# Rounding 64-bit weights in the first block: the sum of the fraction's two parts, by GpSimd instead of VectorE

## The chip, the core and the metric

The kernel runs on one core of a Trainium2 chip. The metric is the device time of one execution in microseconds (us). The kernel before takes 1938.52 us, the median of six runs between 1937.91 and 1939.37 us.

The engines have short names in the profile. PE is TensorE (matrix products), DVE is VectorE, ACT is ScalarE, POOL is GpSimd. SP only issues DMAs here. Each engine works through its own instructions strictly in the order in which the program lists them. An instruction that has to wait for another engine therefore holds up everything behind it on its own engine.

## What is computed

```python
def _attn_ref(x):                      # x: 8 x 3008 x 256, float32
    X = np.fft.fft(x, axis=1)
    X = np.fft.fft(X, axis=2)
    return X.real.astype(np.float32)

def _moe_ref(x, w_in, w_out):          # x: 24064 x 256, w_in: 256 x 2048, w_out: 2048 x 256
    h = x @ w_in
    r = np.maximum(h, 0.0)
    g = r * r
    return (g @ w_out).astype(np.float32)
```

The second function is applied to the first one's output. The two weight matrices are multiplied by a numpy scalar when they are made and so arrive as 64-bit floats. The kernel rounds them to 32-bit floats itself, on the chip.

## The kernel before

The Fourier transform along the 256 columns is folded into `w_in`: the kernel multiplies `w_in` by a cosine and a sine table once and keeps the products in `G1` and `G2`. The transform along the 3008 rows is made per batch (8 batches) with matrix products and folds; its results are `Pt`, `Qt` and `Et`.

The main loop has 384 steps: 8 batches, 6 blocks of 251 (the last 250) columns, and 8 steps j in each block, for 8 pairs of 128 rows of the hidden layer. A step `i` does this:

- `front` (L664 to L670): for each half h, PE makes two products `ph` (L664, L665); DVE adds a term `he` (L667, with `gE`, a factor for each hidden row) and forms the sum and the difference in `g` (L669, L670).
- `combine`: ACT squares the positive part of `g` (L679, L680). From the second block on, POOL also forms four sums `s` (L687 to L690).
- `back`, for step `i-2`: PE multiplies by `wout` (L704 in the first block, L717 later). It needs `wout` of that step in its rounded form.

The first block (steps 0 to 7) also prepares the weights, one slice of `w_in` and one of `w_out` (each 128 x 512 values) per step, because all later blocks reuse them. This is `weights()`, which with `begin_win`, `load_wout` and `leftover` writes the order out by hand. In step `i` the engines get, after the `front` of that step:

1. PE: the products `pg` of `w_in` slice `i+1` with the two tables (L290); ACT copies them to `G1` and `G2` (L291).
2. The first half of rounding (`convert`) for `w_out` slice `i-1`.
3. The second half (`finish`) for `w_in` slice `i+2`, called by `rounded`.
4. The first half for `w_in` slice `i+3`, by `begin_win`.
5. The second half for `w_out` slice `i-1`, by `leftover`, and then `gE` for step `i+1` (L301), which DVE needs for the next step's `he`.

There are exceptions at the ends. Slices 0 and 1 of `w_in` are rounded before the loop. The first half of `w_in` slice 2 also starts there. In step 5 no more `w_in` begins. Step 6 rounds two `w_out` slices (5 and 6), and step 7 begins the last one, which step 8 finishes.

`convert` takes 64-bit floats as pairs of 32-bit words, `high` and `low`, which lie alternately in the tile `raw`. The first half cuts the exponent out of `high` (L262, DVE) and turns it into a 32-bit float's exponent (L264, L265, ACT), cuts the fraction's upper 20 bits out of `high` and sets the leading one (L267, DVE, to the tile `m`), and scales `low` to the fraction's lower part in place (L269, ACT). The second half puts the sign to the exponent (L272), adds the two parts of the fraction (L274) and multiplies fraction and exponent into the destination (L275), all on DVE. Tiles come from pools: three for `m`, two for the exponent, and six in three pools for `raw`. The load of a later slice into a `raw` tile waits until its last reader is done.

POOL's own queue holds, before the loop of the second block, only two DMA issues (L647, L648). They send a part of `Qt` round through DRAM into `Et`, which steps from the second block on use. `awake` is a row of idle matrix products that keeps PE busy during the start.

Of the kernel before, what the change touches and what calls it, by code (L numbers as in the profile page):

```python
# [11 lines left out]
ALU = mybir.AluOpType  # L12
# [70 lines left out]
def kernel(  # L83
# [12 lines left out]
    nc = tc.nc  # L96
# [27 lines left out]
    op = ctx.enter_context(tc.tile_pool(name="op", bufs=2))  # L124
# [5 lines left out]
    tt = nc.vector.tensor_tensor  # L130
# [70 lines left out]
    for i in range(2):  # L201
        nc.vector.tensor_scalar(out=signs[:, i:i + 1], in0=last, scalar1=(-2.0, 2.0)[i], scalar2=(1.0, -1.0)[i],
                                op0=ALU.mult, op1=ALU.add)
# [15 lines left out]
    def pair_in(j):  # L219

        return moe_w_in.rearrange("(c p) (h j f) -> j c p h f", p=P, j=NJ, h=2)[j]
# [5 lines left out]
    def parts(w, k):  # L227
        return w.rearrange("p c (e h) -> p h (c e)", h=k)
# [6 lines left out]
    def scratch():  # L235

        return sp.tile([P, 4 * CK], F32, name="m", tag="s")[:, 0:2 * CH].rearrange("p (c e) -> p c e", c=2)

    def load(src):

        nonlocal raws
        pool, tag = (gp, "g") if raws in (1, 2) else (xp, "x") if raws % (NX + 1) else (ep, "c")
        raws += 1
        single = src.dtype == F32
        raw = pool.tile([P, 2, CH, 1 if single else 2], src.dtype if single else U32, name="raw", tag=tag)
        for c in range(2):
            nc.sync.dma_start(out=raw[:, c].rearrange("p (o e) w -> p o (e w)", o=src.shape[2]),
                              in_=src[c] if single else src[c].bitcast(U32))
        return raw

    def convert(dst, raw):


        k = dst.shape[1]
        if raw.dtype == F32:
            return lambda: nc.vector.tensor_copy(dst, parts(raw[:, :, :, 0], k))
        low, high = raw[:, :, :, 0], raw[:, :, :, 1]
        m = scratch()
        e = fp.tile([P, 2, CH], F32, name="fd", tag="fd")
        mb, eb, rest = m.bitcast(U32), e.bitcast(U32), low.bitcast(F32)  # L260

        nc.vector.tensor_scalar(out=eb, in0=high, scalar1=20, scalar2=0x7FF,  # L262
                                op0=ALU.logical_shift_right, op1=ALU.bitwise_and)
        act(e, eb, AF.Relu, bias=ramp[:, 0:1], scale=-1.0)  # L264
        act(eb, e, AF.Relu, bias=ramp[:, 1:2], scale=-2.0 ** 23)  # L265

        nc.vector.tensor_scalar(out=mb, in0=high, scalar1=0xFFFFF, scalar2=0x100000,  # L267
                                op0=ALU.bitwise_and, op1=ALU.bitwise_or)
        act(rest, low, AF.Copy, scale=2.0 ** -32)  # L269

        def finish():
            nc.vector.scalar_tensor_tensor(out=eb, in0=high, scalar=0x80000000, in1=eb,  # L272
                                           op0=ALU.bitwise_and, op1=ALU.bitwise_or)
            tt(out=m, in0=mb, in1=rest, op=ALU.add)  # L274
            nc.vector.scalar_tensor_tensor(out=dst, in0=parts(m, k), scalar=2.0 ** -20, in1=parts(e, k),  # L275
                                           op0=ALU.mult, op1=ALU.mult)

        return finish


    def begin_win(j):

        w = ep.tile([P, 2, CH], F32, name="win", tag="sB" if j % 2 else "sA")
        finish = convert(parts(w, 1), win.pop(j, None) or load(pair_in(j)))

        def products():
            for tab, G, nm in ((cosd, G1, "mC"), (sind, G2, "mD")):
                pg = psm.tile([P, CH], F32, name="pg", tag=nm)
                for i in range(2):
                    nc.tensor.matmul(pg, tab[:, i], w[:, i], start=i == 0, stop=i == 1)  # L290
                nc.scalar.copy(G.rearrange("p (h j f) -> j p h f", h=2, j=NJ)[j],  # L291
                               pg.rearrange("p (h f) -> p h f", h=2))

        def for_e():

            ps = psd.tile([P, CH], F32, name="pe", tag="d")
            for h in range(2):
                fc = j + NJ * h
                nc.tensor.matmul(ps[:, h:h + 1], G2[:, fc * P:(fc + 1) * P], last, start=True, stop=True)

            return lambda: nc.vector.tensor_scalar_mul(gE[:, j::NJ], ps[:, 0:2], 0.5)  # L301

        win[j] = finish, products, for_e

    win = {}

    def load_wout(j):

        return convert(wout[:, j].rearrange("p h c e -> p h (c e)"), load(pair_out(j)))
# [533 lines left out]
    for_q(0)  # L843
    for_p(1)
    begin_win(0)
    load_x(0, 2)
    load_x(0, 3)
# [37 lines left out]
    q_part("odd0", "odd1", "odd2")  # L885
    copy_e = win[0][2]()
    begin_win(1)
    for_q(3)
    q_part("even0", "even1", "even2")
    awake(12)  # L890
    rounded(1)
    for kp in range(2):
        for nm in ("join_4", "join_2", "lo"):
            groups[1, kp, nm]()
        if kp == 0:
            begin_win(2)
# [44 lines left out]
    for i in range(len(steps) + LAG + 4):  # L941
        if i < len(steps):
            b, k0, n, j = steps[i]
# [96 lines left out]
```

## Time and profile before

| what | value |
|---|---|
| median of 6 runs | 1938.52 us |
| the profiled execution's own time | 1941.41 us |
| its span, first to last instruction | 1939.6 us |
| busy share of the span: PE, DVE, ACT, POOL | 99%, 73%, 48%, 61% |
| busy POOL instructions between 3.2 and 109.5 us | two DMA issues, 1.25 us |
| PE busy from 113.6 to 151.0 us (37.4 us long) | 37.40 us |
| mean granted TensorE clock | 0.997 of full speed |

The span is the distance from the first to the last instruction in one profiled execution; 1.8 us of that execution's own time lie outside it. A row of the timeline gives the start in us, the duration in us, the engine, the line of the code, the operation, the tiles and shapes (partitions x elements) and, in square brackets, how long the engine had stood idle before and what ended that. Durations of neighbours on one engine overlap a little: an instruction starts before the one ahead of it has drained. What an instruction takes away from its engine is therefore the distance from its start to the next start.

### The profile page before, as it was taken

How to read it: one execution, taken by the hardware profiler on the slowest of the kernel's cores; microseconds unless marked ns; L12 is line 12 of the kernel's file. 1: busy time of each engine (PE TensorE's matmuls, PEld its weight loads, DVE VectorE, ACT ScalarE, POOL GpSimd, SP SyncE). 2: the span in 40 equal slices, each digit the busy share in tenths (PEclk: the TensorE clock that was granted, in tenths of full speed). 3: DMA queues.
4: the chain of work that ended last, by engine and by line, in shares of the span. 5: the costliest groups of instructions: out<-in, count | busy, mean ns of one | idle time of the engine just before them, and what ended most of it. 6: DMA issues, size and time to landing. Idle time of an engine off the chain costs nothing.

```text
span 1939.6 us, 27913 instructions
## 1 busy us (share of the span) xinstructions
PE 1925.6 (99%) x9266; PEld 1711.9 (88%) x9266; DVE 1424.0 (73%) x3502; ACT 939.5 (48%) x1134; POOL 1184.1 (61%) x1708
## 2 busy tenths in 40 slices
PE   8999999999999999999999999999999999999999
PEld 7788888888988899888998889888898888988887
DVE  7998867777677876787667876777767787655554
ACT  2755544454445544544444454445544554444444
POOL 0047746776567665766566765666756676566655
PEclk9999999999999999999999999999999999999999
DMA  7332101111011100111011100111001100000000
GB/s 211 112 45 52 37 9 52 33 28 31 28 40 31 38 12 27 41 40 29 11 36 40 42 20 11 40 49 28 20 16 53 33 11 22 28 12 11 22 11 22
DMA packets 145783, 69.56 MB, mean 36 GB/s; under 512 B 129309, under 2 KB 136423, under 8 KB 145638
## 3 DMA queue, kind: packets, MB, share of 16 engines
q1 hardware_dynamic: 145186, 66.87, 13.3%
q8 instruction: 73, 1.20, 0.3%
q14 instruction: 72, 0.59, 0.1%
q0 software_dynamic: 176, 0.65, 0.1%
q10 hardware_dynamic: 276, 0.26, 0.0%
HBM read 43.03 MB, written 24.69 MB: 35 GB/s over the span
## 4 chain that ended last, share of the span: by engine, by line
PE 95%; DVE 3%; DMA 1%; issue 0%; SPq 0%; ACT 0%; DVEq 0%
PE ph L664 16%; PE ph L665 16%; PE mC L717 16%; PE mA L717 16%; PE mB L717 16%; PE mD L717 8%; PE pd L578 2%; PE pd L501 2%; DVE m L274 0%; DMA cosT<-in_cos_s_dram 0%; DMA sind<-in_sin_d_dram 0%; DVE he L667 0%; DVE fd L272 0%; DVE g L670 0%; PE mA L704 0%
## 5 line engine op out<-in xcount | busy, mean ns | idle before, releaser
L679 ACT ACTIVATE g<-g 128x1004 f32<-128x1004 f32 (+1 forms) x384 | 399.4, 1040 | 783.5 <-DVE g L670 424.4
L667 DVE SCALAR_TENSOR_TENSOR he<-Et,gE,ph 128x251 f32<-128x251 f32 (+1 forms) x768 | 361.6, 471 | 385.8 <-PE ph L665 382.7
L687 POOL TENSOR_TENSOR s<-g 128x251 f32<-128x251 f32 (+1 forms) x376 | 248.6, 661 | 641.9 <-ACT g L680 506.0
L664 PE MATMUL ph<-Pt,G 128*128 128x251 f32 (+1 forms) x1536 | 451.9, 375 | 0.2 <-DVE g L670 0.2
L665 PE MATMUL ph<-Qt,G 127*128 127x251 f32 (+1 forms) x1536 | 451.3, 374 | 0.0
L680 ACT ACTIVATE g<-g 128x1004 f32<-128x1004 f32 (+1 forms) x384 | 399.3, 1040 | 12.2
L717 PE MATMUL mC<-s,wsum 128*128 128x251 f32 (+1 forms) x1504 | 381.4, 374 | 0.0
L717 PE MATMUL mA<-g,wout 128*128 128x251 f32 (+1 forms) x1504 | 379.9, 374 | 0.0
L669 DVE TENSOR_TENSOR g<-he,ph 128x251 f32<-128x251 f32 (+1 forms) x768 | 320.6, 417 | 54.5 <-DVE he L667 0.9
L665 PEld LDWEIGHTS ph<-Qt,G 127*128 127x128 f32 x1536 | 291.3, 190 | 35.8
L664 PEld LDWEIGHTS ph<-Pt,G 128*128 128x128 f32 x1536 | 286.7, 189 | 36.2 <-DVE dc L547 1.3
L717 PEld LDWEIGHTS mC<-s,wsum 128*128 128x128 f32 x1504 | 285.5, 190 | 34.5
L670 DVE TENSOR_TENSOR g<-he,ph 128x251 f32<-128x251 f32 (+1 forms) x768 | 314.2, 409 | 0.0
L717 PEld LDWEIGHTS mA<-g,wout 128*128 128x128 f32 x1504 | 282.6, 189 | 35.0 <-issue 0.3
L689 POOL TENSOR_TENSOR s<-g 128x251 f32<-128x251 f32 (+1 forms) x376 | 302.8, 805 | 0.0
L688 POOL TENSOR_TENSOR s<-s,g 128x251 f32<-128x251 f32 (+1 forms) x376 | 279.6, 744 | 29.5
L690 POOL TENSOR_TENSOR s<-g,s 128x251 f32<-128x251 f32 (+1 forms) x376 | 260.2, 692 | 0.0
L717 PE MATMUL mB<-g,wsum 128*128 128x251 f32 (+1 forms) x752 | 220.5, 374 | 0.0
L717 PE MATMUL mD<-s,wout 128*128 128x251 f32 (+1 forms) x752 | 220.3, 374 | 0.0
L717 PE MATMUL mB<-s,wout 128*128 128x251 f32 (+1 forms) x752 | 220.0, 374 | 0.0
L717 PEld LDWEIGHTS mB<-g,wsum 128*128 128x128 f32 x752 | 142.5, 190 | 17.5
L717 PEld LDWEIGHTS mD<-s,wout 128*128 128x128 f32 x752 | 141.9, 189 | 17.7
(139 smaller groups left out, 1359.1 us busy)
## 6 DMA issues: line engine op xcount, KB each, us to landing
out_dram<-os SPq DMA_DIRECT2D x376, 56.0 KB
xt<-in_x_dram SPq DMA_DIRECT2D x25, 384.0 KB
xt<-in_x_dram SPq DMA_DIRECT2D x63, 128.0 KB
Et<-e_dram SPq DMA_DIRECT2D x7, 752.5 KB
xt<-in_x_dram SPq DMA_DIRECT2D x9, 512.0 KB
out_dram<-os SPq DMA_DIRECT2D x288, 6.8 KB
raw<-in_moe_w_in_dram SPq DMA_DIRECT2D x16, 256.0 KB
raw<-in_moe_w_out_dram SPq DMA_DIRECT2D x16, 256.0 KB
```

Source lines behind the costliest of these rows:

```text
L664: nc.tensor.matmul(hP, G1[:, fs], pt[:, ks], start=True, stop=True)
L665: nc.tensor.matmul(hQ, G2[0:P - 1, fs], qt[0:P - 1, ks], start=True, stop=True)
L667: nc.vector.scalar_tensor_tensor(out=t, in0=et[:, ks], scalar=gE[:, fc:fc + 1], in1=hP, op0=ALU.mult, op1=ALU.add)
L669: tt(out=g[:, h, 0, 0:n], in0=t, in1=hQ, op=ALU.add)
L670: tt(out=g[:, h, 1, 0:n][:, ::-1], in0=t, in1=hQ, op=ALU.subtract)
L679: act(v, v, AF.Relu)
L680: act(v, v, AF.Square)
L687: gt(out=s1, in0=g21, in1=g22, op=ALU.add)
L688: gt(out=s2, in0=s1, in1=g11, op=ALU.subtract)
L689: gt(out=s3, in0=g11, in1=g21, op=ALU.subtract)
L690: gt(out=s4, in0=g12, in1=s2, op=ALU.subtract)
L717: nc.tensor.matmul(acc[nm][:, i, 0:n], w, v[:, 0:n], start=j == 0 and i == 0, stop=j == NJ - 1, skip_group_check=True)
```

## The change

The fraction's upper part gets another leading pattern: instead of the integer with a one at bit 20, DVE sets the exponent bits of a float of size 2^23, so that `m` can be read as the float 2^23 plus the 20 bits. The constant 2^20 - 2^23 then has to be added to get the former value. For 14 of the 16 slices (all but `w_in` slices 0 and 1) POOL adds this constant in place and then adds the lower part, both in the first half of the rounding. The addition in the second half (L274) is left out there. For the two slices that are rounded before the loop, DVE does both additions in one instruction in the second half. Line numbers grow by 7 behind the change; in the changed file the two new POOL lines are L271 and L274, and the former L269, L272 and L275 are L272, L277 and L282.

```diff
-    def convert(dst, raw):
+    def convert(dst, raw, ahead=True):
...
-        nc.vector.tensor_scalar(out=mb, in0=high, scalar1=0xFFFFF, scalar2=0x100000,
+
+        nc.vector.tensor_scalar(out=mb, in0=high, scalar1=0xFFFFF, scalar2=0x4B000000,
                                 op0=ALU.bitwise_and, op1=ALU.bitwise_or)
+        if ahead:
+            nc.gpsimd.tensor_scalar_add(m, m, 2.0 ** 20 - 2.0 ** 23)
         act(rest, low, AF.Copy, scale=2.0 ** -32)
+        if ahead:
+            nc.gpsimd.tensor_tensor(out=m, in0=m, in1=rest, op=ALU.add)
 
         def finish():
             nc.vector.scalar_tensor_tensor(out=eb, in0=high, scalar=0x80000000, in1=eb,
                                            op0=ALU.bitwise_and, op1=ALU.bitwise_or)
-            tt(out=m, in0=mb, in1=rest, op=ALU.add)
+            if not ahead:
+                nc.vector.scalar_tensor_tensor(out=m, in0=m, scalar=2.0 ** 20 - 2.0 ** 23, in1=rest,
+                                               op0=ALU.add, op1=ALU.add)
             nc.vector.scalar_tensor_tensor(out=dst, in0=parts(m, k), scalar=2.0 ** -20, in1=parts(e, k),
                                            op0=ALU.mult, op1=ALU.mult)
...
-        finish = convert(parts(w, 1), win.pop(j, None) or load(pair_in(j)))
+        finish = convert(parts(w, 1), win.pop(j, None) or load(pair_in(j)), j > 1)
```

## Prediction

> **What bounds the kernel now.** I read the page's busy shares and its chain first: 95% of the span is PE's, and the lines changed hold almost nothing. So the question is only what the start does to PE. The table by stretches tells where PE stops waiting; its columns after the stretch's length are the busy times of PE, PEld, DVE, ACT and POOL.
>
> ```profile
> 68.39:76.31 7.92, 7.53 (x37) 6.41 (x38) 7.64 (x17) 6.53 (x11) 0.00 (x0) 1.00 0.42 134
> 113.60:151.00 37.40, 37.40 (x178) 33.24 (x177) 33.81 (x88) 18.71 (x19) 23.23 (x35) 1.00 0.41 41
> ```
>
> Step 3 (first row) leaves PE idle for 0.4 us; behind the first block PE is never idle. So a microsecond by which the first block's last products come earlier or later is a microsecond of the whole time. PE's waits between 46 and 114 us give the most that can be won:
>
> ```profile
> PE pe L299 <- ACT G L291: 2.7, 2, 2.3
> PE mA L704 <- DVE wout L275: 1.5, 4, 0.6
> PE pe L642 <- DVE Qt L538: 1.5, 1, 1.5
> ```
>
> The third lies ahead of the changed part. The other two sum to 4.2 us, the ceiling of any gain. Who sets the step? Here is DVE in the second part of step 3, starts and durations in us:
>
> ```profile
> 70.72 0.42 DVE L262 TENSOR_SCALAR fd<-raw 128x512 uint32<-128x512 uint32 x1
> 71.06 0.42 DVE L267 TENSOR_SCALAR m<-raw 128x512 uint32<-128x512 uint32 x1
> 71.39 0.68 DVE L272 SCALAR_TENSOR_TENSOR fd<-raw,fd 128x512 uint32<-128x512 uint32 x1
> 71.99 0.68 DVE L274 TENSOR_TENSOR m<-m,raw 128x512 f32<-128x512 uint32 x1
> 72.71 0.69 DVE L275 SCALAR_TENSOR_TENSOR win<-m,fd 128x512 f32<-128x512 f32 x1
> 73.44 0.43 DVE L262 TENSOR_SCALAR fd<-raw 128x512 uint32<-128x512 uint32 x1
> 73.78 0.42 DVE L267 TENSOR_SCALAR m<-raw 128x512 uint32<-128x512 uint32 x1
> 74.11 0.69 DVE L272 SCALAR_TENSOR_TENSOR fd<-raw,fd 128x512 uint32<-128x512 uint32 x1
> 74.72 0.68 DVE L274 TENSOR_TENSOR m<-m,raw 128x512 f32<-128x512 uint32 x1
> 75.44 0.69 DVE L275 SCALAR_TENSOR_TENSOR wout<-m,fd 128x512 f32<-128x512 f32 x1
> 76.05 0.15 DVE L301 TENSOR_SCALAR gE<-pe 128x2 f32<-128x2 f32 x1
> ```
>
> No row has idle time before it, and PE's `mA` at 76.19 waits for the last L275. DVE is the bound: 7.92 us from one `he` (68.39) to the next (76.31). PE comes next: its step took 7.27 us where it did not wait (L664 at 57.15 to 64.42).
>
> **The gain.** 13 L274 in the loop go. A pair L272, L274 takes 0.60 + 0.72 us from start to start; without L274, L275 waits for L272 instead and keeps the 0.12 us of that dependency, so each is worth 0.60 us, 1.20 in a full step. The two slices left on DVE swap one 0.68 us instruction for another with two tile operands in SBUF, as L272 is (0.68): nothing. POOL stands idle there, 59.88 us before 109.58, so the 28 new instructions displace nothing. The order of the built programs confirms the count (1713 to 1741 on POOL, 14 fewer on DVE); that the change does not do what it says is excluded.
>
> **What POOL's instructions take.** Memsets give its price per column: 128x196 took 0.26 us and 128x1792 1.59, so 0.10 fixed and 0.83 ns a column. A sum of 128x251 takes 0.63 (L687): 0.53/251 = 2.1 ns a column, hence 1.08 + 0.10 = 1.18 us for 512. The add of a constant does not occur. Its ends are a memset's 0.53 (it also has to read) and the sum's 1.18 (one operand less). The nearest row, one operand in and out, is the affine select, 0.29 for 128 columns: 1.5 ns a column, 0.87 us. I take that.
>
> The Trainium skill (GPSIMD Engine Reference, "Elementwise — side-by-side cycle accounting") gives a tight loop over 512 elements as 769 ns measured; with that the sum below would be 4.6 instead of 5.6. Its "Engine selection" says not to put elementwise work on GpSimd at all.
>
> **Where they meet DVE.** Later blocks show both engines together. L422 is twice a sum of two SBUF tiles:
>
> ```profile
> 153.14 0.91 POOL L688 TENSOR_TENSOR s<-s,g 128x251 f32<-128x251 f32 x1
> 153.50 1.69 DVE L422 TENSOR_TENSOR w<-sc 94x256 f32<-94x256 f32 x2
> 154.01 0.90 POOL L689 TENSOR_TENSOR s<-g 128x251 f32<-128x251 f32 x1
> 154.87 0.81 POOL L690 TENSOR_TENSOR s<-g,s 128x251 f32<-128x251 f32 x1
> 193.88 0.76 DVE L422 TENSOR_TENSOR w<-sc 128x256 f32<-128x256 f32 x2
> ```
>
> Beside POOL they took 1.69, else 0.76: 0.93 more, two of POOL's 0.53 us stretches less the gaps between DVE's own instructions. They take turns, one at a time. L667 to L670, with an operand in PSUM, keep 0.41 to 0.48 whether POOL works or not. So L272 and L275 will exclude POOL's work, and the 2.6 us of front instructions and `gE` will not.
>
> L262 and L267 never met POOL. They do 512 columns in 0.42 where L272 needs 0.68. I count them as excluded too, like L272, and free as the other end. The skill's SBUF page ("SBUF — State Buffer", "Who interferes with whom") says that a `tensor_scalar` in the two-port mode takes the pair of ports shared with GpSimd; that favours the first end, and the sum stays 5.6 by it.
>
> **A full step, followed through.** POOL's order is add and sum of `wout`, then add and sum of `win`.
> 1. The add for `wout` becomes ready when L267 ends, just as L272 begins. It goes next, and L275 of `win` starts its work behind it: 0.77 less the 0.17 us gap, +0.60.
> 2. The sum for `wout` waits for ACT's L269 (which ends 2.2 us after L267 began). It falls on the second L262: 1.08 - 0.16, +0.92.
> 3. The add for `win` follows its L267 and cuts in ahead of the second L275: +0.60.
> 4. The sum for `win` runs beside the front of the next step: nothing. Its L275 comes a step later.
> Together 2.1 us for 1.20 saved: **+0.9 per full step**, and since DVE sets the step, PE's wait grows by it.
>
> Step by step: step 0 has only L275 of slice 2, whose pair is done by 47 us, 3 us ahead: -0.6. Step 1: ACT's rest comes behind L679, L680 and two copies, ending 58.6 before, 58.0 now; the sum then ends at 59.2, L272 (0.53 of work) at 59.7, the waiting add at 60.5, L275 at 61.0, where 60.2 - 0.6 was the mark: +1.5. Steps 2 to 4: 3 x 0.9. Step 5 begins no `win`, one add and one sum: -1.2 + 0.6 + 1.0 = +0.4. Step 6 rounds two `wout` slices back to back: from ACT's first rest (96.24) DVE took 3.33 us to `gE`. Now sum (1.2), add (0.8), L275 (0.6), the other sum (1.1), L272 and L275 (1.2) are in line: 4.9, +1.6. The last slice has a full step before its use: 0. The sum is -0.6 + 1.5 + 2.7 + 0.4 + 1.6 = **+5.6 us**.
>
> Set against the profiled execution: span 1939.6 to 1945.2, own time 1941.41 to 1947.0. That execution lies 2.9 us above the median, and the difference carries over: 1938.52 + 5.6 = **1944.1 us**.
>
> **What else moves, at nothing.** POOL's DMA issues L647 and L648 stand behind the pair of slice 2, which ends by 47 us, when L647 started anyway (46.99); `Et` is used from 102.84 on, so 50 us cover it. Loads into `raw` now wait for POOL's sum, not for L274; no L262 waited for one by more than 0.1 us in all, and sums end at about L274's old times. The `xt` loads (97.02) behind them are first read at 113.99.
>
> **Bounds.** Ten adds lie on the path (two in steps 1 to 4, one each in 5 and 6): at 0.53 the sum falls by 10 x 0.34 to +2.2, at 1.18 it rises by 3.1 to +8.7. A sum at twice the longer row (2 x 0.72 = 1.44) adds 7 x 0.26, to +10.5. If L262 and L267 do not exclude POOL, step 2 above costs little: 0.7 less in each of steps 2 to 4, 0.4 in step 1, giving +3.1.
>
> **Rivals.** *POOL works beside DVE* (not slower): should neither L272 nor L275 exclude an add or sum of these shapes, DVE's step falls to 7.92 - 1.20 = 6.7 and PE's 7.27 becomes the bound: 4 x -0.66 in steps 2 to 5, -0.6 in step 0, and +1.2 in steps 1 and 6, where L275 still waits for ACT and then 1.2 us of sum: -2.0, or 1936.5. The point from which it decides: a mean cost of a full step's exclusion under 1.2 us. For it: POOL is free and 13 instructions go; against it: the rows at 153.50. With everything in time, -4.2. *POOL's add is far dearer* (slow form, or its code has to be fetched on first use): at 2.0 us, 10 x 1.13 more, +17 or 1955. Against it: the affine select's 0.29 includes any such cost; for it: nothing here shows this form.
>
> **How the numbers follow.** About 0.2%, 3.9 us, is what a measurement of this kernel can tell from no change. Exclusion with the priced rows: 0.72, of which 0.2 lies under +3.9. Beside each other: 0.20, hardly ever under -3.9. Dear add: 0.08. So faster 0.03, same 0.38, slower 0.59. The range goes from -1.5 (most of the first rival) to +11 (the upper bounds): 1937.0 to 1949.5. The forecast case alone: 1940.7 to 1949.0.
>
> **What would show it.** Right: L275 of `win` and the second L262 or L267 at 1.2 to 1.7 us instead of 0.42 to 0.69; `he` to `he` 8.8 us in steps 2 to 4; PE's wait ahead of `mA` at 1.3 us in each of these steps instead of 0.39; POOL's add near 0.87, sum near 1.18. Wrong: L275 at 0.69 beside POOL and steps of 7.3, or an add over 1.5 us.

## The result, and the profile after

The changed kernel takes 1943.02 us, the median of 18 runs, against 1938.26 us for the kernel before (36 runs): 4.8 us more, a ratio of 1.0025 with a 95% interval of 1.0019 to 1.0032. The forecast was 1944.1, and 0.59 of the chance lay on slower.

The two profiled executions show less of it in their spans, 1941.5 against 1939.6 us, because the one of before started its loop late: its first `he` stands at 47.34 us, the one after at 44.27. Between 20 and 30 us its granted clock was 0.66, against 1.00 in the one after. That execution of before also took 2.9 us more than its median. The comparison is therefore made from the first `he` (step 0) to that of step 9: 60.94 us before, 65.68 after, 4.74 more. Step 9 gives 0.28 of that back (4.26 us after 4.54): PE's first product with `s` in the second block comes 67.83 us behind the first `he` before and 72.29 after, 4.46 more. Trace and medians thus agree within 0.3 us. From 113.6 us on, PE is again busy for 37.40 of 37.40 us, so nothing is won or lost later.

The view of PE's waits between 46 and 122 us, with the sum in us, how often and the longest:

```profile
PE mA L711 <- DVE wout L282: 4.2, 4, 1.8
PE pe L306 <- ACT G L298: 2.2, 2, 1.7
PE ph L671 <- DVE g L677: 0.3, 1, 0.3
```

The wait for rounded `wout` was 1.5 us before; it is 4.2 now (0.40, 1.01 and 1.01 in steps 2 to 4, and 1.76 in step 6). The wait for the `G` copies fell by 0.5 (step 0, the gain). DVE in step 3, from the timeline (start, duration):

```profile
69.06 0.42 DVE L262 TENSOR_SCALAR fd<-raw 128x512 uint32<-128x512 uint32 x1
69.39 0.42 DVE L268 TENSOR_SCALAR m<-raw 128x512 uint32<-128x512 uint32 x1
69.72 0.68 DVE L277 SCALAR_TENSOR_TENSOR fd<-raw,fd 128x512 uint32<-128x512 uint32 x1
70.52 0.90 DVE L282 SCALAR_TENSOR_TENSOR win<-m,fd 128x512 f32<-128x512 f32 x1
71.46 0.58 DVE L262 TENSOR_SCALAR fd<-raw 128x512 uint32<-128x512 uint32 x1
71.96 1.50 DVE L268 TENSOR_SCALAR m<-raw 128x512 uint32<-128x512 uint32 x1
73.38 0.69 DVE L277 SCALAR_TENSOR_TENSOR fd<-raw,fd 128x512 uint32<-128x512 uint32 x1
74.18 0.90 DVE L282 SCALAR_TENSOR_TENSOR wout<-m,fd 128x512 f32<-128x512 f32 x1
75.00 0.15 DVE L308 TENSOR_SCALAR gE<-pe 128x2 f32<-128x2 f32 x1
```

And POOL beside it, from the same timeline:

```profile
69.89 1.86 POOL L271 TENSOR_SCALAR m<-m 128x512 f32<-128x512 f32 x1 [1.65 <-DVE m L268]
71.84 1.34 POOL L274 TENSOR_TENSOR m<-m,raw 128x512 f32<-128x512 f32 x1
73.55 1.86 POOL L271 TENSOR_SCALAR m<-m 128x512 f32<-128x512 f32 x1 [0.37 <-DVE m L268]
75.50 1.30 POOL L274 TENSOR_TENSOR m<-m,raw 128x512 f32<-128x512 f32 x1
```

DVE has no idle time in this step; its instructions have become longer. L268 at 71.96 takes 1.50 us instead of 0.42 and ends 0.28 after POOL's sum (71.84 to 73.18), that is, it does most of its work behind it. Both L282 take 0.90 instead of 0.69 beside POOL's add, and the second L262 0.58 instead of 0.42. The step, from start to start: the two L274 gone, -0.53 each (L277 to L282 is 0.80 where L272, L274 and L275 took 1.33); +0.21 twice, +0.16 and +1.09: +0.61. Measured: 8.55 - 7.92 = +0.63.

Steps 2 to 4, which are of this kind, add 1.9 us in all. The larger part, 3.1 us, lies in steps 1, 5 and 6, and there DVE does stand idle; step 0 gains 0.5. The view of DVE's waits between 46 and 122 us has one line for POOL, and before it has none; its four waits are in steps 1, 5 and 6 (twice):

```profile
DVE wout L282 <- POOL m L274: 4.9, 4, 1.3
56.90 1.09 DVE L282 SCALAR_TENSOR_TENSOR wout<-m,fd 128x512 f32<-128x512 f32 x1 [1.18 <-POOL m L274]
90.30 0.69 DVE L282 SCALAR_TENSOR_TENSOR wout<-m,fd 128x512 f32<-128x512 f32 x1 [1.19 <-POOL m L274]
97.47 1.09 DVE L282 SCALAR_TENSOR_TENSOR wout<-m,fd 128x512 f32<-128x512 f32 x1 [1.30 <-POOL m L274]
100.34 0.69 DVE L282 SCALAR_TENSOR_TENSOR wout<-m,fd 128x512 f32<-128x512 f32 x1 [1.18 <-POOL m L274]
```

So the loss has two parts: instructions made longer by POOL, and waits for POOL's sum where it starts late (in step 1, behind ACT's L272) or little of DVE's work stands ahead of L282 (steps 5 and 6). The two mix: in step 1 the sum that DVE waits for takes 1.72 us instead of 1.29. The granted clock was 0.82 in step 1 of this execution, but that doesn't make the wait: `wout_only`, below, has it at 1.00 too (1.19 us before its L282).

### The profile page after: what moved, and what is told of

Same layout as the page of the kernel before. It is cut to its first block, busy times and chain, and to the rows that moved or that the text cites. A ratio compares the mean times of both kernels' runs of the same rounds, so it can differ in the third digit from the quotient of the medians.

```text
span 1941.5 us, 27977 instructions
## 1 busy us (share of the span) xinstructions
PE 1925.5 (99%) x9266; PEld 1710.7 (88%) x9266; DVE 1424.8 (73%) x3488; ACT 939.5 (48%) x1134; POOL 1226.0 (63%) x1736
## 4 chain that ended last, share of the span: by engine, by line
PE 95%; POOL 1%; DMA 1%; DVE 1%; issue 1%; ACT 1%; SPq 0%; DVEq 0%; POOLq 0%
PE ph L671 16%; PE mC L724 16%; PE ph L672 16%; PE mA L724 16%; PE mB L724 16%; PE mD L724 8%; PE pd L585 2%; PE pd L508 1%; POOL m L271 1%; POOL m L274 1%; DMA cosT<-in_cos_s_dram 0%; DMA cosd<-in_cos_d_dram 0%; DMA xt<-in_x_dram 0%; DVE he L674 0%; PE mB L711 0%
```

## The experiments

The port theory: POOL and DVE take turns at SBUF, so POOL's instructions lengthen those of DVE that have no operand in PSUM. (The runs show such turns; the port itself no run shows.) The lateness theory: DVE only waits for POOL's results, which come late behind ACT. Each edit below is made to the changed kernel. The table gives the time from one step's first `he` to the next one's, for the steps 0 to 6, then the sum from step 0 to step 9 in the profiled execution, and the ratio of the times to the kernel before.

| kernel | 0 | 1 | 2 | 3 | 4 | 5 | 6 | 0 to 9 | ratio, 95% interval |
|---|---|---|---|---|---|---|---|---|---|
| before | 5.19 | 7.93 | 7.93 | 7.92 | 7.93 | 7.16 | 8.44 | 60.94 | |
| the change | 4.66 | 9.24 | 8.55 | 8.55 | 8.54 | 7.37 | 10.04 | 65.68 | 1.0025, 1.0019 to 1.0032 |
| dve_both | 5.20 | 7.93 | 8.38 | 7.93 | 7.92 | 7.13 | 8.43 | 61.36 | 1.0000, 0.9991 to 1.0010 |
| no_sum | 4.59 | 7.11 | 6.72 | 6.73 | 7.01 | 7.27 | 7.91 | 56.91 | 0.9984, 0.9975 to 0.9994 |
| add_alone | 4.66 | 7.45 | 7.45 | 7.44 | 7.44 | 6.76 | 7.98 | 58.68 | 0.9988, 0.9978 to 0.9997 |
| sum_alone | 4.66 | 8.42 | 7.98 | 8.00 | 7.98 | 7.20 | 9.66 | 62.60 | 1.0014, 1.0004 to 1.0023 |
| win_only | 4.67 | 8.34 | 7.82 | 7.83 | 7.83 | 6.61 | 8.44 | 60.00 | 0.9997, 0.9988 to 1.0006 |
| wout_only | 5.20 | 8.89 | 8.78 | 8.77 | 8.78 | 8.13 | 10.06 | 67.35 | 1.0036, 1.0022 to 1.0049 |
| win_front | 4.67 | 7.93 | 7.35 | 7.36 | 7.35 | 6.69 | 8.44 | 59.03 | 0.9990, 0.9981 to 0.9999 |
| act_add_win | 4.67 | 8.40 | 7.42 | 7.40 | 7.42 | 6.61 | 8.44 | 59.54 | 0.9994, 0.9986 to 1.0003 |

### dve_both: the new pattern without POOL

```diff
-    def convert(dst, raw, ahead=True):
+    def convert(dst, raw, ahead=False):
...
-        finish = convert(parts(w, 1), win.pop(j, None) or load(pair_in(j)), j > 1)
+        finish = convert(parts(w, 1), win.pop(j, None) or load(pair_in(j)))
```

> All slices take the path that the change keeps for two of them: float with a leading 2^23, both additions by DVE in one instruction, nothing on POOL. Port theory (POOL and DVE take turns at SBUF) and lateness theory (DVE only waits for POOL's results to arrive) alike: as before, 1938 us within 1, steps of 7.9 us from he to he. If the new leading pattern itself cost something, steps over 8.1.

1939.19 us and steps of 7.93, but for one of 8.38, in which PE was busy throughout, at a granted clock of 0.82 (0.76 in the step ahead of it). The leading 2^23 and the two additions in one instruction cost nothing that the interval or the other steps would show. The loss is POOL's part.

### no_sum: DVE's addition gone, and nothing in its place

```diff
-        if ahead:
-            nc.gpsimd.tensor_scalar_add(m, m, 2.0 ** 20 - 2.0 ** 23)
...
-        if ahead:
-            nc.gpsimd.tensor_tensor(out=m, in0=m, in1=rest, op=ALU.add)
```

> Leaves out the constant and the lower part of the fraction for 14 slices: neither POOL nor DVE adds. Ceiling of what DVE's addition is worth. Both theories: DVE's step falls under PE's 7.27 us, PE becomes the bound, 3.6 us less than before (1934.7), PE's waits in the first block some 4 us less; he(0) to he(9) 57 us where before has 60.9.

1935.57 us, 3.4 less than the 1938.92 of the kernel before beside it, as both theories had it. This is the most that moving the addition can bring, and it is under the 4.2 us of PE's waits.

### sum_alone: POOL's sum without the add

```diff
-        if ahead:
-            nc.gpsimd.tensor_scalar_add(m, m, 2.0 ** 20 - 2.0 ** 23)
```

> Leaves out the constant 2^20 - 2^23: POOL does only its sum of two tiles. Port theory: the sum, now ready earlier, shuts DVE out for its whole 1.3 us twice in a step, ahead of L277 and ahead of L282 of w_out, so steps 2 to 4 are even longer than with both (9.2 us against 8.55) and the time is 5.3 us over before (1943.6). Lateness theory: the sum's result comes 1.5 us earlier than with the add ahead of it, steps at 7.2 us, 1.5 us under before (1936.8). Plain adding up of shares: between, about +3.

1940.60 us, 1.7 more than before, and steps of 7.98: neither 9.2 nor 7.2. The rows of one step, DVE and POOL from the timeline:

```profile
62.34 1.78 DVE L275 SCALAR_TENSOR_TENSOR fd<-raw,fd 128x512 uint32<-128x512 uint32 x1
64.23 0.69 DVE L280 SCALAR_TENSOR_TENSOR wout<-m,fd 128x512 f32<-128x512 f32 x1
62.12 1.45 POOL L272 TENSOR_TENSOR m<-m,raw 128x512 f32<-128x512 f32 x1 [4.02 <-DVE fd L262]
64.30 1.78 POOL L272 TENSOR_TENSOR m<-m,raw 128x512 f32<-128x512 f32 x1 [0.73 <-ACT raw L270]
```

The sum for `w_out` (62.12) shuts L275 (the former L272) out, 1.78 instead of 0.68, as the port theory says. The sum for `w_in` was expected to do the same to L280. But L280 started at 64.23, 0.07 us ahead of it, and kept 0.69, while the sum took 1.78 instead of 1.29. In these rows who starts first goes first, and the other waits its turn. So one exclusion per step instead of two: -0.53 x 2 + 1.10 = +0.04 a step, as measured (7.98 against 7.93). The expectation failed on 0.07 us of order, not on the mechanism. Lateness alone is ruled out: nothing that L275 needs comes from POOL. But lateness has its share: in steps 1, 5 and 6, L280 waits for POOL's sum four times, 4.9 us together, and the loss of this kernel lies in steps 1 and 6 (+0.49 and +1.22), with only 0.2 in steps 2 to 4.

### add_alone: POOL's add without the sum

```diff
-        if ahead:
-            nc.gpsimd.tensor_tensor(out=m, in0=m, in1=rest, op=ALU.add)
```

> Leaves out the lower part of the fraction: POOL adds only the constant, 1.5 us on POOL. Port theory, refined by the trace after (the add takes the read port for about 0.45 of its 1.5 us): L282 and one mask instruction 0.2 us longer, steps 7.4 us, PE nearly the bound, 3 to 3.6 us under before (1935). If the add shut DVE out for its whole 1.5 us: steps of 9 us, +5. Lateness theory: as no_sum, -3.6.

1936.30 us, 2.6 less than before, and steps of 7.45: L280 (the former L275) takes 0.90 and the second L262 0.58 beside an add of 1.79 us. The add is longer than the sum, yet it holds DVE up for only 0.2 us at a time. The two parts don't add up: the add alone wins 2.6, the sum alone loses 1.7, both together lose 4.8. Counted from `no_sum`, which has no addition for these slices, that is 0.7, 5.0 and 8.1 us. The add ahead of the sum delays it, to where it shuts out L268, and it takes its own turns besides.

### win_only and wout_only: POOL for one of the two matrices

```diff
-    def convert(dst, raw, ahead=True):
+    def convert(dst, raw, ahead=False):
```

> POOL's pair only for the w_in slices; w_out slices are added by DVE. Port theory: the sum runs beside the front of the next step, the add still costs DVE's own addition for w_out 0.4 us, so a full step is 7.8 us and the time 0.5 us under before. If each half carried half the loss, +2.4. Without any exclusion: steps 7.4, -2.3.

```diff
-        finish = convert(parts(w, 1), win.pop(j, None) or load(pair_in(j)), j > 1)
+        finish = convert(parts(w, 1), win.pop(j, None) or load(pair_in(j)), False)
```

> POOL's pair only for the w_out slices. Port theory: the loss is all here; the sum for w_out still shuts DVE out for 1.1 us and steps 5 and 6 and 1 keep their wait behind ACT, while DVE keeps its addition for w_in: steps 8.9 us, 6.8 us over before, more than with both halves. If each half carried half the loss, +2.4. Without exclusion: steps 7.4, +1.

`win_only` takes 1938.45 us, 0.4 less than the kernel before beside it (1938.86), within its interval; its steps are 7.83, as expected. `wout_only` takes 1945.88, 7.0 more, with steps of 8.78. The loss is all with `w_out`, whose sum is needed in the same step and falls on DVE's rounding (the second L262 takes 1.39 us beside it, and L282 waits for it three times in steps 1 and 6, 3.7 us together); the sum for `w_in` has a step to spare and runs beside the front. In `win_only` DVE waits for POOL nowhere; the add lengthens DVE's own addition for `w_out` from 0.69 to 1.10 us. `wout_only` is slower than the whole change mainly because there DVE keeps one addition more, which takes 1.10 us beside the add too.

### win_front: POOL's pair moved to the front

```diff
-    def convert(dst, raw, ahead=True):
+    def convert(dst, raw, ahead=False, hold=False):
...
-        nc.vector.tensor_scalar(out=mb, in0=high, scalar1=0xFFFFF, scalar2=0x4B000000,
-                                op0=ALU.bitwise_and, op1=ALU.bitwise_or)
-        if ahead:
-            nc.gpsimd.tensor_scalar_add(m, m, 2.0 ** 20 - 2.0 ** 23)
+        def fraction():
...
+        def low_part():
...
+        if not hold:
+            fraction()
         act(rest, low, AF.Copy, scale=2.0 ** -32)
-        if ahead:
-            nc.gpsimd.tensor_tensor(out=m, in0=m, in1=rest, op=ALU.add)
+        if not hold:
+            low_part()
+        else:
+            held_back.append(lambda: (fraction(), low_part()))
+            late.append(release)
...
+            release()
             nc.vector.scalar_tensor_tensor(out=dst, in0=parts(m, k), scalar=2.0 ** -20, in1=parts(e, k),
                                            op0=ALU.mult, op1=ALU.mult)
...
+        finish = convert(parts(w, 1), win.pop(j, None) or load(pair_in(j)), j > 1, j > 2)
```

`fraction` holds the mask and POOL's add, `low_part` POOL's sum; `release` calls what is held back, ahead of the next L282.

> As win_only, but the mask instruction of the w_in slice, and with it POOL's pair, is moved to stand ahead of the last multiplication for w_out, so that POOL works while DVE runs the front, whose operands lie in PSUM. Port theory: steps 2 to 4 at 7.4 us, 2.2 us under before. Lateness theory: the results come later than in win_only but are needed a step later, so no different from win_only.

1937.42 us, ratio 0.9990 (0.9981 to 0.9999): 1.4 us less than before, the fastest of those that leave nothing out, by a hair that its interval just resolves. From `win_only` its interval does not separate it; the steps do. Steps 2 to 4 are 7.35, close to PE's 7.27. One pair of POOL, a DVE row of the front beside it, and the DVE row that it lengthens, from the timeline:

```profile
64.12 1.86 POOL L278 TENSOR_SCALAR m<-m 128x512 f32<-128x512 f32 x1 [4.11 <-DVE m L275]
66.06 1.30 POOL L282 TENSOR_TENSOR m<-m,raw 128x512 f32<-128x512 f32 x1
66.82 0.41 DVE L695 TENSOR_TENSOR g<-he,ph 128x251 f32<-128x251 f32 x1
67.15 0.50 DVE L268 TENSOR_SCALAR fd<-raw 128x512 uint32<-128x512 uint32 x1
```

The same 3.2 us of POOL now cost DVE 0.08 us, at L268. Against `win_only` nothing changed but the place of the mask instruction and, with it, the time at which POOL works. That is the port theory's point, and lateness had no difference here.

### act_add_win: ACT adds the constant

```diff
-    def convert(dst, raw, ahead=True):
+    def convert(dst, raw, ahead=False):
...
-        if ahead:
-            nc.gpsimd.tensor_scalar_add(m, m, 2.0 ** 20 - 2.0 ** 23)
         act(rest, low, AF.Copy, scale=2.0 ** -32)
+        if ahead:
+            act(m, m, AF.Copy, bias=2.0 ** 20 - 2.0 ** 23)
```

> As win_only, but ACT adds the constant (0.6 us of its slack per step) and POOL only sums. Port theory: the sum alone runs beside the front, steps 2 to 4 at 7.4 us, 1.5 us under before (step 1 loses 0.6 to ACT, which is late there). If ACT becomes the bound: steps of 7.9, no gain.

1937.84 us, 1.0 less than before where 1.5 was expected, with an interval that includes no change. Steps 2 to 4 are 7.4 and step 1 is 8.40, as expected.

### add_halves: what the add's 1.48 us are made of

```diff
-            nc.gpsimd.tensor_scalar_add(m, m, 2.0 ** 20 - 2.0 ** 23)
+            for c in range(2):
+                nc.gpsimd.tensor_scalar_add(m[:, c], m[:, c], 2.0 ** 20 - 2.0 ** 23)
```

> The change, with POOL's add of the constant split into two instructions of 256 columns each. If the add's 1.48 us is a price per column on top of POOL's fixed 0.1, each half takes 0.79 us where it stands alone (1.38/512 = 2.7 ns a column); if most of it is a fixed cost of this form, each takes over 1 us and the pair over 2. Port theory: the reading part of each half shrinks to about 0.2 us, so L282 of w_in waits no longer than before, 0.2 us.

```profile
41.41 0.85 POOL L272 TENSOR_SCALAR m<-m 128x256 f32<-128x256 f32 x1
48.63 1.67 POOL L272 TENSOR_SCALAR m<-m 128x256 f32<-128x256 f32 x2 [1.97 <-DVE gE L309]
53.05 0.69 DVE L283 SCALAR_TENSOR_TENSOR win<-m,fd 128x512 f32<-128x512 f32 x1
```

A half takes 0.85 us, a whole add 1.48: (1.48 - 0.85) / 256 = 2.5 ns a column and 0.22 fixed. So it is a price per column; two halves in a row take 1.67. The last row, DVE's multiplication while two halves run (52.43 to 54.55), keeps its 0.69 where it took 0.90 beside the whole add; steps 2 to 4 take 8.25 to 8.29 us against 8.55. One run took 1942.18 us, 4.4 more than one of the kernel before on the same chip.

## Why the prediction was right

The direction and the place were as forecast, the mechanism too for POOL's sum, but not for its add. That the size came within 0.9 us (+4.8 for +5.6) is in part luck. By its terms:

- *The gain of a removed L274*: 0.60 forecast, 0.53 measured. L277's start to that of L282 is 0.80 us, not the 0.60 + 0.12 of the forecast: L282 starts 0.12 us behind the end of L277 (0.68), whereas L274 had started 0.08 ahead of that end.
- *POOL's sum*: 1.18 forecast, 1.28 to 1.30 alone. It shut out a mask instruction for 1.09 us where +0.92 was forecast. The open question whether L262 and L268 are excluded at all is settled by L268 at 1.50. The rule of the Trainium skill ("SBUF — State Buffer", "Who interferes with whom") on a `tensor_scalar` in the two-port mode agrees with that row, though no run shows in which mode L268 ran. The other end, +3.1, would have been too low.
- *POOL's add* was mis-sized twice, in opposite directions. It takes 1.48 us alone and 1.86 in steps 2 to 4, not 0.87: the affine select was a poor neighbour, and the upper bound taken from the sum (1.18) did not hold. The 769 ns that the Trainium skill (GPSIMD Engine Reference, "Elementwise — side-by-side cycle accounting") gives for a tight loop over 512 elements are not reached by this form. But of its 1.48 us it shuts out an instruction with two SBUF operands for only a part: in steps 2 to 4 +0.21 on each L282, plus 0.16 on L262, against +0.60 twice. (Where it starts 0.06 us ahead of L282, in steps 1 and 6, L282 takes 1.09, +0.40.) By its price in the sum, ten adds of 1.48 would have made +11.7, or 1950.2 us, outside the range. The step of the forecast that failed is therefore that POOL holds SBUF for the length of an instruction; it held for the sum, not for the add. The two errors cancelled in part, and that is luck.
- *Steps 0, 1, 5 and 6*: -0.53, +1.31, +0.21 and +1.60 against -0.6, +1.5, +0.4 and +1.6. In steps 1 and 6 the forecast had DVE wait for POOL's sum, and it does. *Steps 2 to 4*: +0.62 each against +0.9. Steps 7 and 8, taken as 0, gave +0.01 and +0.28, and step 9 gave the 0.28 back.
- *The rival of work side by side*: ruled out by `sum_alone` and L268; only beside the front does POOL work for nothing, which `win_front` shows. The sum of this rival had a slip: it let step 5 fall by 0.66 to PE's 7.27, but that step took 7.16 already; without it the rival gives -1.4 instead of -2.0. *The dear add*: 1.48 was dear. By the price of the forecast, 1.41 already leads to the upper end of the range (5.6 + 10 x 0.54 = 11.0); the time stayed inside because most of the add fell where DVE was not held.
- *The signs*: L268 at 1.50 and steps of 8.55 for 8.8 came as said. L282 of `win` did not (0.90 for 1.2 to 1.7), and PE's wait ahead of `mA` was 0.40, 1.01 and 1.01 for 1.3. An add over 1.5 us was named as a sign of being wrong: it was 1.86 beside DVE and 1.48 alone, and the part on the add was wrong.
- *Range*: 1937.0 to 1949.5 held the time.

## What to carry to other kernels

Moving work from a busy engine to an idle one gains only what does not come back, and here more came back than was gained, in two ways. Where the two engines take turns at SBUF, moved microseconds come back as longer instructions, and no row shows them as a wait (steps 2 to 4). Where the result is due at once, the busy engine waits for it, and the view of waits shows it (4.9 us in steps 1, 5 and 6). Look at which of the busy engine's instructions will run at that moment, and place the moved work beside those that take an operand from PSUM. When a result has a whole step until its use, that choice is free; when it is used in the same step (here `w_out`), the runs speak for leaving it where it was.

## What the runs showed of the hardware that was not expected

- A POOL add of a constant over 128x512 takes longer (1.48 us) than a POOL sum of two tiles of that size (1.29), yet costs DVE far less. In the trace after, an L282 that starts within the add waits 0.21 us (0.40 where the add starts just ahead of it), and one L268 beside an add got through in the middle of it:

```profile
94.51 0.83 DVE L268 TENSOR_SCALAR m<-raw 128x512 uint32<-128x512 uint32 x1
94.35 1.59 POOL L271 TENSOR_SCALAR m<-m 128x512 f32<-128x512 f32 x1 [4.08 <-DVE m L268]
```

  This L268 ended at 95.34 and the add at 95.94, while the L262 at 71.46 above waited until near the end of its add (71.75). Reading in the add's first half microsecond, then computing, and writing at its end would fit both. No run took these phases apart, so that stays an inference.
- Between two ready instructions, 0.07 us of lead decided who went first (`sum_alone`: L280 at 64.23 and 72.22 us, POOL's sum at 64.30 and 72.29). By the price of the other exclusion in that step, the reverse order would have cost some 1.1 us more; no run shows it.
